# V of the first four tiles from x as loaded, and a new order of the V stage, in a fused attention and SwiGLU kernel

## The chip, the cores and the metric

The kernel runs on one core of one Trainium2 chip. Time is device time in microseconds of one execution; lower is better. A core has a matmul engine (PE, whose weight loads are shown as PEld), a vector engine (DVE), a scalar engine (ACT), GpSimd (POOL), and SyncE (SP), which here issues every DMA.

## What is computed

x has 2048 tokens of 640 elements, bf16. It is normalised once, and two branches are added to it: a linear attention with 32 heads of 20 elements and the feature map phi, and a SwiGLU with 1536 hidden columns.

```python
def _A_ref(x, wqkv, w_phi, wo):
    qkv = ...                      # x @ wqkv as q, k, v of (B, H, S, Dh)
    pq = jnp.einsum("bhsd,hdf->bhsf", q, w_phi)
    pk = jnp.einsum("bhsd,hdf->bhsf", k, w_phi)
    phi_q = jnp.concatenate([_softmax(pq), _softmax(-pq)], axis=-1)
    phi_k = jnp.concatenate([_softmax(pk), _softmax(-pk)], axis=-1)
    kv = jnp.einsum("bhsf,bhsd->bhfd", phi_k, v)
    z  = jnp.einsum("bhsf->bhf", phi_k)
    num = jnp.einsum("bhqf,bhfd->bhqd", phi_q, kv)
    den = jnp.einsum("bhqf,bhf->bhq", phi_q, z)[..., None] + 1e-6
    return ... (num / den) ... @ wo

def _B_ref(x, w1, w3, w2):
    return jnp.einsum("bsf,fd->bsd", _silu(x @ w1) * (x @ w3), w2)

xn = _layernorm(x)                 # (x - mean) / sqrt(var + 1e-5) over the 640
return x + _A_ref(xn, A_wqkv, A_w_phi, A_wo) + _B_ref(xn, B_w1, B_w3, B_w2)
```

## The kernel before

**Tiles and stages.** The tokens are 16 tiles of 128 rows. The order in which each engine meets its instructions is written out by hand: the engines run their own lists in order, and wait for one another by semaphores. Each operation below appends its instructions to the lists of the engines that it uses. The stages are named here after the first product that each makes.

- *V stage* (lines 642 to 734): x is loaded, normalised and transposed into `xnT` (640 elements as 5 chunks of 128 partitions, tokens along the row); V is computed tile by tile into `vaug`; six units of the SwiGLU are done between; and w_phi is folded into the K weights (`FB(d)`, five blocks, into `wkphi`).
- *K stage* (lines 737 to 749): 16 turns, one tile each. `phi_unit` makes ten matmuls `pk`, six exponentials on ACT, sums and reciprocals on DVE, and the division on POOL; `kv_unit` adds phi and V of the tile two turns back into `acc`; `fill` runs SwiGLU units. In turns 4 to 8 `fuse` folds w_phi into the Q weights.
- *Q stage* (lines 753 to 782): the same with `pq`; SwiGLU units in its first four turns, then the output of a tile per turn. SP transposes phi and o by DMA.

**Normalising a tile.** `ln_stats` (DVE, two bn_stats and one bn_aggr) gives mean and variance in `mv`. For tiles 0 to 3 `ln_root` takes a square root on ACT and `lx` begins with a reciprocal on DVE. For the others `ln_pow` and `ln_newton` make `rstd` on POOL, six small instructions for a pair of tiles. `ln_x` then writes (x - mean) * rstd in place, on DVE, or on ACT for tiles 12 and 13 (`BY_ACT`).

**Transposing a tile.** `T` is `x_transposed`. Tiles 0 to 3: five PE transposes into one PSUM bank and two copies by ACT into `xnT`. Tiles 4 to 15: one DMA transpose on SP. Each is behind its `ln_x`.

**V of a tile.** `V(t)` is ten matmuls at L304 (five chunks, each with 360 and 280 output columns in two banks), and three copies by ACT (L319) into `vaug`, which holds a column of ones ahead of each group of three heads.

**A SwiGLU unit** (sc, fi) is 512 tokens by 128 hidden columns: five matmuls into a bank `gp`, five into `up`, 512 columns each; a tanh on ACT; and two products on DVE (L436 reads `gp`, L439 reads `up`). `glu_half` makes half of the tokens. There are 48 units; the list `glu` gives their order, hidden columns 0 to 511 of all tokens first.

**PSUM.** Eight banks: one pair (`pair`, `two`), and six that are handed out as they come free (`bank`). An instruction that takes a bank waits for the last reader of its former content.

**SP** issues the loads in the order written, first x of tiles 0 and 1, then the V weights `wv` in three loads, then x of tiles 2 and 3. The first columns of w1 and w3 wait for a small POOL copy behind the root of tile 0 (L644), x of tiles 4 to 11 for one behind that of tile 1 (L649). The K weights come transposed by DMA in five pieces (`ldT(wkT, 1, d)`), one for each `FB(d)`. `wkT`, `wqT` and `wv` are the three parts of `reg_w`; `wo` is loaded over `wkT` when it is free.

Before tile 0 is there PE multiplies zeros (`warm(WARM)`, 44 matmuls of 128x128).

Of the kernel before, what the change touches and what calls it, by code (L numbers as in the profile page):

```python
# [8 lines left out]
P = 128  # L9
# [3 lines left out]
def kernel(  # L13
# [32 lines left out]
    BY_ACT = (12, 13)  # L46
    WARM = 44
# [52 lines left out]
    )  # L100
    vaug = reg_v[:, 0 : NST * NCH * VC].rearrange("p (t c e) -> p t c e", t=NST, e=VC)
# [11 lines left out]
    wide = one.tile([P, H * 21], f32, name="wide")  # L113

# [12 lines left out]
    with tc.manual_schedule():  # L127
# [20 lines left out]
        ld_wv(0, 1)  # L148
        ld_wv(1, 2)
        ld_wv(3, 2)  # L150
# [59 lines left out]
        def ln_stats(t, between=None):  # L210
            xt = xin[:, (t // 4) % 3, t % 4, :]
            st = work.tile([P, 2, 6], f32, name="st")
            for i in range(2):
                nc.vector.bn_stats(out=st[:, i, :], in_=xt[:, i * HD : (i + 1) * HD])  # L214
                if i == 0 and between:
                    between()
            nc.vector.bn_aggr(out=mv[:, t, :], in_=st[:])

        ry = one.tile([P, NST], f32, name="ry")
        shift = one.tile([P, NST], f32, name="shift")  # L220
# [16 lines left out]
        def ln_newton(t, n):  # L237

            r = slice(t, t + n)
            eng = nc.gpsimd  # L240
            if n == 1:
                eng.tensor_scalar(
                    out=rstd[:, r], in0=ry[:, r], scalar1=ve[:, r], scalar2=ry[:, r],
                    op0=ALU.mult, op1=ALU.mult,
                )
            else:
                eng.tensor_mul(out=rstd[:, r], in0=ry[:, r], in1=ry[:, r])
                eng.tensor_mul(out=rstd[:, r], in0=rstd[:, r], in1=ve[:, r])
            eng.tensor_scalar(
                out=rstd[:, r], in0=rstd[:, r], scalar1=-0.5, scalar2=1.5,  # L250
                op0=ALU.mult, op1=ALU.add,
            )
            eng.tensor_mul(out=rstd[:, r], in0=rstd[:, r], in1=ry[:, r])
            if t in BY_ACT:
                eng.tensor_scalar(
                    out=shift[:, r], in0=mv[:, r, 0], scalar1=rstd[:, r], scalar2=-1.0,
                    op0=ALU.mult, op1=ALU.mult,
                )

        def ln_x(t):  # L260
            xt = xin[:, (t // 4) % 3, t % 4, :]
            if t in BY_ACT:
                nc.scalar.activation(
                    out=xt, in_=xt, func=AF.Identity,
                    scale=rstd[:, t : t + 1], bias=shift[:, t : t + 1],
                )
                return
            nc.vector.tensor_scalar(
                out=xt, in0=xt, scalar1=mv[:, t, 0:1], scalar2=rstd[:, t : t + 1],
                op0=ALU.subtract, op1=ALU.mult,  # L270
            )

        def x_transposed(*ts, between=None):

            for t in ts:
                xn = xin[:, (t // 4) % 3, t % 4, :]
                if t >= BY_DMA:
                    nc.sync.dma_start_transpose(out=xnT[:, :, t * P : (t + 1) * P], in_=xn)
                    continue
                ps = bank("pst", bf)  # L280
                for c in range(KD):
                    nc.tensor.transpose(  # L282
                        ps[:, c * P : (c + 1) * P], xn[:, c * P : (c + 1) * P], ident[:]
                    )
                for c0, c1 in ((0, 2), (2, KD)):
                    nc.scalar.copy(  # L286
                        out=xnT[:, c0:c1, t * P : (t + 1) * P],
                        in_=ps[:, c0 * P : c1 * P].rearrange("p (c s) -> p c s", s=P),
                    )
                    if c0 == 0 and between:  # L290
                        between()
# [4 lines left out]
        def by_token(cols, w, name, cut, between=(KD, None)):  # L296

            ps = [bank(name), bank(name)]
            for c in range(KD):
                if c == between[0]:  # L300
                    between[1]()
                for i in range(2):
                    a, b = (0, cut) if i == 0 else (cut, D)
                    nc.tensor.matmul(  # L304
                        ps[i][:, 0 : b - a],
                        xnT[:, c, cols],
                        w[:, c, a:b],
                        start=(c == 0),
                        stop=(c == KD - 1),
                        skip_group_check=True,  # L310
                    )
            return ps

        def v_unit(dst, cols, between=(KD, None)):
            for piece in chunks(by_token(cols, wv, "pv", CH, between)):
# [102 lines left out]
        def glu_half(i, sc, fi, gp, up, between=None):  # L418

            for ps, w in ((gp, w1), (up, w3)):  # L420
                for c in range(KD):
                    nc.tensor.matmul(  # L422
                        ps[:, i * 256 : (i + 1) * 256],
                        w[:, c, fi * P : (fi + 1) * P],
                        xnT[:, c, sc * 512 + i * 256 : sc * 512 + (i + 1) * 256],
                        start=(c == 0),
                        stop=(c == KD - 1),
                        skip_group_check=True,
                    )
                if between:  # L430
                    between()
                between = None
# [175 lines left out]
        def stats(t0, n):  # L608
            for t in range(t0, t0 + n):
                ln_stats(t)  # L610
# [20 lines left out]
        def V(t, between=(KD, None)):  # L631
            v_unit(vaug[:, t], tile_of(t), between)
# [8 lines left out]

        ln_stats(0)
        ln_root(0)
        nc.gpsimd.tensor_copy(out=w1[0:1, 0, 0:1], in_=ry[0:1, 0:1])  # L644
        ld_glu(0, 256)
        ln_stats(1, between=lambda: lx(0, 1))
        T(0, between=lambda: ln_root(1))
        warm(4)
        nc.gpsimd.tensor_copy(out=xin[0:1, 1, 0, 0:1], in_=ry[0:1, 1:2])  # L649
        ld_tiles(4, 2)  # L650
        ld_tiles(6, 2)
        ld_tiles(8, 2)
        ld_tiles(10, 2)
        ld_glu(256, 512)
        ld(wps[:], A_w_phi.rearrange("h j f -> (h j) f").rearrange("(c p) f -> p c f", p=P))
        lx(1, 1)
        ln_stats(2)

        def second():
            T(1)  # L660
            ln_root(2)

        V(0, between=(4, second))
        ln_stats(3, between=lambda: lx(2, 1))
        pieces = list(chunks(by_token(tile_of(1), wv, "pv", CH)))
        v_copy(vaug[:, 1], *pieces[0])
        ln_root(3)


        first = (*glu.pop(0), *two("g0"))  # L670
        glu_half(0, *first, between=lambda: T(2))
        for piece in pieces[1:]:
            v_copy(vaug[:, 1], *piece)
        lx(3, 1)
        V(2, between=(3, lambda: T(3)))
        nc.scalar.activation(out=table[:], in_=nought[:, 0:1], func=AF.Tanh)
        ld_tiles(12, 4)
        ldT(wkT, 1, 0)
        pieces = list(chunks(by_token(tile_of(3), wv, "pv", CH)))
        stats(4, 2)  # L680
        stats(6, 2)
        glu_half(1, *first)
        g0 = glu_done(*first)
        for piece in pieces:
            v_copy(vaug[:, 3], *piece)
        lx(4, 2)
        T(4, 5)
        g1 = unit()
        g0()
        lx(6, 2)  # L690
        T(6, 7)
        ldT(wkT, 1, 1)
        stats(8, 1)
        stats(9, 1)
        g2 = unit()
        g1()
        lx(8, 1)
        T(8)
        g3 = unit(two("g3"))
        g2()  # L700
        lx(9, 1)
        T(9)
        ldT(wkT, 1, 2)
        V(4)
        V(5)
        stats(10, 2)
        g3()
        V(6)
        V(7)
        stats(12, 1)  # L710
        stats(13, 1)
        g4 = unit()
        lx(10, 2)
        T(10, 11)
        V(8)
        g4()
        stats(14, 2)
        lx(12, 1)
        T(12)
        V(9)  # L720
        g5 = unit()
        lx(13, 1)
        T(13)
        ldT(wkT, 1, 3)
        V(10)
        phi_blocks()
        g5()
        lx(14, 2)
        T(14, 15)
        ldT(wkT, 1, 4)  # L730
        V(11)
        ld_glu(512, F)
        nc.sync.dma_start_transpose(out=wqT, in_=A_wqkv[:, 0:D])
        V(12), FB(0), FB(1), V(13), FB(2), V(14), FB(3), V(15), FB(4)


        acc = pair("pkv")
        for t in range(NST):
            phi_unit(t, wkphi, "pk")
            if t > 1:  # L740
                kv_unit(t - 2, vaug[:, t - 2], acc, t == 2, False)
            if t:
                fill(1)
            if 4 <= t < 9:
                fuse(wqphi, wqT, t - 4, [bank("pf"), bank("pf")])
            fill(1)
            if t >= 12:
                norm_unit(wkphi, 0, t - 12)
# [4 lines left out]
        for t in range(NST + 4):  # L753
            if t < NST:
                phi_unit(t, wqphi, "pq")
            if t < 2:
                kv_unit(NST - 2 + t, vaug[:, NST - 2 + t], acc, False, t == 1)
# [3 lines left out]
            if t < 4:  # L761
                fill(3 if t else 2)
# [74 lines left out]
```

## Time and profile before

| | us |
|---|---|
| median of 3 runs | 270.27 (269.98 to 270.28) |
| span of the profiled execution | 268.56 |
| PE busy | 263.1 |
| DVE busy | 188.7 |
| ACT busy | 111.6 |
| POOL busy | 95.6 |
| first transpose of tile 0 on PE | 5.72 |
| first matmul of the K stage | 44.62 |
| first matmul of the Q stage | 139.67 |

The times of the table come from one profiled execution, but for the first row; its span ends with the last instruction, and the runs' median lies 1.71 us above it. The views used below list groups of instructions: the start in us from the span's start, the time from the start of the first to the end of the last of the group, the engine, the line of the kernel, the operation with what it writes and reads (out<-in), the count, and in brackets the idle time of the engine before it with what ended it. Matmuls overlap: the time of a group of them includes the tail of the last one.

### The profile page before, as it was taken

The page shows a single profiled execution, that of the slowest core. Times are in us where ns is not written, and L with a number is a line of the kernel's source. Part 1 is how long each engine was busy: PE and PEld are TensorE (multiplying, and loading weights), DVE is VectorE, ACT ScalarE, POOL GpSimd, SP SyncE. Part 2 cuts the span into 40 slices and gives each one's busy share as a digit, 9 for nine tenths or more (in the row PEclk, how much of TensorE's full clock was granted, in tenths as well). Part 3 has the DMA queues.
Part 4 walks back from the last instruction along what each step waited for, and adds up shares of the span by engine and source line. Part 5 has one row for each costly group of instructions (what it writes and reads, how often), then busy time and mean ns, then how long its engine had stood idle before and what let it go on. Part 6 is the DMA issues. An engine that isn't in the chain of part 4 may idle for free.

```text
span 268.6 us, 5257 instructions
## 1 busy us (share of the span) xinstructions
PE 263.1 (98%) x1979; PEld 167.9 (63%) x1996; DVE 188.7 (70%) x348; ACT 111.6 (42%) x342; POOL 95.6 (36%) x99
## 2 busy tenths in 40 slices
PE   8999999999999999999999999999999999999995
PEld 8656667555555555555555445677777777777773
DVE  4899950887776667777777788876766777776341
ACT  2673668544555554346656545422222222221000
POOL 5054740354433333334444321333344444433000
PEclk9999999999999999999999999999999999999999
DMA  6998347970000000000000874355556655556831
GB/s 213 324 219 147 84 100 208 278 200 2 0 0 2 0 4 0 0 4 0 0 2 0 240 164 99 75 136 128 130 133 125 151 128 128 129 144 136 155 98 55
DMA packets 62909, 27.81 MB, mean 104 GB/s; under 512 B 49952, under 2 KB 61600, under 8 KB 62880
## 3 DMA queue, kind: packets, MB, share of 16 engines
q1 hardware_dynamic: 62880, 27.43, 42.2%
q8 instruction: 17, 0.28, 0.4%
q14 instruction: 12, 0.10, 0.1%
HBM read 12.81 MB, written 2.62 MB: 57 GB/s over the span
## 4 chain that ended last, share of the span: by engine, by line
PE 97%; ACT 1%; issue 0%; DVE 0%
PE acc L547 28%; PE up L404 19%; PE gp L404 18%; PE pv L304 8%; PE pq L304 8%; PE pk L304 8%; PE pr L484 2%; PE pkv L449 2%; PE idle L193 2%; PE pf L388 1%; PE g L422 1%; PE g L404 1%; PE pst L282 1%; ACT reg_v L319 0%; ACT xnT L286 0%
## 5 line engine op out<-in xcount | busy, mean ns | idle before, releaser
L370 POOL TENSOR_TENSOR phi<-phi,rk 128x1320 bf16<-128x1320 bf16 x32 | 77.3, 2415 | 133.4 <-DVE rk L369 94.8
L367 DVE TENSOR_REDUCE sk<-phi 128x66 f32<-128x1320 bf16 x32 | 48.9, 1528 | 40.8 <-ACT phi L333 39.7
L404 PEld LDWEIGHTS <-w 128*128 128x128 bf16 x470 | 44.6, 98 | 49.4
L304 PEld LDWEIGHTS <-xnT 128*128 128x128 bf16 x480 | 45.3, 98 | 21.6 <-ACT xnT L286 1.6
L404 PE MATMUL up<-xnT,w 128*128 128x512 bf16 x227 | 57.0, 379 | 0.3
L404 PE MATMUL gp<-xnT,w 128*128 128x512 bf16 x216 | 55.9, 378 | 0.6
L547 PE MATMUL acc<-reg_v,reg_h 128*128 128x320 bf16 (+2 forms) x384 | 54.9, 299 | 0.0
L333 ACT ACTIVATE phi<-pq 128x360 bf16<-128x360 f32 (+2 forms) x96 | 24.8, 364 | 58.0 <-issue 44.1
L547 PEld LDWEIGHTS <-reg_h 128*128 128x128 bf16 x384 | 37.3, 98 | 14.4
L415 ACT ACTIVATE th<-gp 128x512 f32<-128x512 f32 x46 | 27.7, 603 | 30.2 <-PE gp L404 29.7
L439 DVE SCALAR_TENSOR_TENSOR reg_h<-gs,up 128x512 bf16<-128x512 bf16 x46 | 31.7, 688 | 5.1 <-PE pk L304 0.5
L333 ACT ACTIVATE phi<-pk 128x360 bf16<-128x360 f32 (+2 forms) x96 | 24.8, 364 | 24.1 <-PE pk L304 24.1
L436 DVE SCALAR_TENSOR_TENSOR gs<-th,gp 128x512 bf16<-128x512 f32 x46 | 30.2, 658 | 0.0
L556 DVE TENSOR_TENSOR res<-acc,xr 128x320 bf16<-128x320 f32 (+2 forms) x32 | 14.3, 487 | 20.3 <-PE acc L547 20.3
L304 PE MATMUL pk<-wkphi,xnT 128*128 128x360 bf16 (+1 forms) x160 | 24.5, 299 | 0.0
L547 PE MATMUL acc<-reg_w,reg_v 128*128 128x320 bf16 (+2 forms) x160 | 24.5, 299 | 0.0
L304 PE MATMUL pq<-wqphi,xnT 128*128 128x360 bf16 (+1 forms) x160 | 24.3, 299 | 0.0
L304 PE MATMUL pv<-reg_w,xnT 128*128 128x360 bf16 (+1 forms) x160 | 23.7, 300 | 0.4 <-ACT xnT L286 0.4
L369 DVE RECIPROCAL rk<-sk 128x66 f32<-128x66 f32 x32 | 18.1, 566 | 3.2
L547 PEld LDWEIGHTS <-reg_v 128*128 128x128 bf16 x160 | 15.7, 98 | 6.1
L319 ACT CAST reg_v<-pv 128x360 bf16<-128x360 f32 (+2 forms) x48 | 13.3, 354 | 6.5 <-PE pv L304 6.3
L214 DVE BATCH_NORM_STATS2 st<-reg_h 128x6 f32<-128x320 bf16 x32 | 13.9, 470 | 2.0 <-DMA reg_h<-in_A_x_dram 2.0
(72 smaller groups left out, 145.6 us busy)
## 6 DMA issues: line engine op xcount, KB each, us to landing
w<-in_B_w_dram SPq DMA_DIRECT2D x2, 1280.0 KB, 8.7
xr<-in_A_x_dram SPq DMA_DIRECT2D x16, 160.0 KB, 2.5
out_dram<-res SPq DMA_DIRECT2D x15, 160.0 KB, 1.8
reg_v<-in_B_w_dram SPq DMA_DIRECT2D x1, 1920.0 KB, 9.1
w<-in_B_w_dram SPq DMA_DIRECT2D x4, 320.0 KB, 5.6
reg_h<-in_A_x_dram SPq DMA_DIRECT2D x4, 320.0 KB, 4.7
reg_w<-in_A_wo_dram SPq DMA_DIRECT2D x1, 800.0 KB, 4.6
reg_h<-in_A_x_dram SPq DMA_DIRECT2D x4, 160.0 KB, 3.6
```

The source lines that it names most:

```text
L214: nc.vector.bn_stats(out=st[:, i, :], in_=xt[:, i * HD : (i + 1) * HD])
L304: nc.tensor.matmul(ps[i][:, 0 : b - a], xnT[:, c, cols], w[:, c, a:b], start=(c == 0), stop=(c == KD - 1), skip_group_check=True,)
L333: nc.scalar.activation(out=dst[:, c0 : c0 + n, g, 0:k], in_=p.rearrange("p (c f) -> p c f", c=n), func=AF.Exp, scale=1.0 - 2.0 * g,)
L367: nc.vector.reduce_sum(out=sk[:], in_=rows, axis=AX.X)
L369: nc.vector.reciprocal(out=rk[:], in_=sk[:])
L370: nc.gpsimd.tensor_mul(out=rows, in0=rows, in1=rk[:, :, :, None].to_broadcast([P, 2 * NCH, 3, Dh]))
L404: nc.tensor.matmul(ps, w[:, c, fi * P : (fi + 1) * P], xnT[:, c, sc * 512 : (sc + 1) * 512], start=(c == 0), stop=(c == KD - 1),)
L415: nc.scalar.activation(out=th[:], in_=gp, func=AF.Tanh, scale=0.5)
L436: nc.vector.scalar_tensor_tensor(out=gs[:], in0=th[:], scalar=1.0, in1=gp, op0=ALU.add, op1=ALU.mult)
L439: nc.vector.scalar_tensor_tensor(out=hT[:, 4 * sc : 4 * sc + 4, fi, :], in0=gs[:].rearrange("p (t s) -> p t s", t=4), scalar=0.5, in1=up.r ...
L547: nc.tensor.matmul(ps[:, 0 : b - a], rows[j][0], rows[j][1][:, a:b], start=(j == 0), stop=(j == len(rows) - 1),)
L556: nc.vector.tensor_tensor(out=res[:, a:b], in0=ps[:, 0 : b - a], in1=xr[:, a:b], op=ALU.add)
```

## The change

The V weights act on x as loaded for tiles 0 to 3: V = rstd * (x @ wv) - rstd * mean * (column sums of wv). So these tiles are transposed by PE without being normalised (`by_pe(xrT, t)`, into the part of `reg_w` that later holds `wqT`), multiplied (`raw_part`), and scaled by rstd into `v_raw`, on DVE for tile 0 and on ACT for tiles 1 to 3. The second term is added in the K stage: wv is loaded a second time, transposed, over `wkT`; in turns 4 to 8 ACT sums its rows with a minus sign (`column_sum`); SP writes the 640 sums to DRAM and reads them back to all partitions (`less_sum`); in turns 10 to 13 DVE adds them, times `drift` = mean * rstd, to `v_raw` into `vaug` (`raw_centred`). The K stage therefore takes tiles 4 to 15 first and 0 to 3 last.

For the SwiGLU and for K and Q the tiles 0 to 3 are still normalised and transposed: 0, 1 and 3 by PE a second time, tile 2 by DMA. 19 matmuls of zeros are left of 44 ahead of the first transpose. The V stage has eight SwiGLU units in place of six, the first two by halves side by side, and turns 2 and 3 of the Q stage one unit less each. Tiles 12 and 13 are normalised on DVE like the others. `ln_stats` of two tiles makes its four bn_stats before its two bn_aggr. The V weights come in five loads; the loads of w1, w3, x, w_phi and the transposed K weights have a new order, and so have the units, tiles and blocks of the V stage. V of every second tile takes the pair of banks.

```diff
-    BY_ACT = (12, 13)
-    WARM = 44
+    WARM = 19
+    RAW = 4
...
+    xrT = reg_w[:, KD * D : KD * D + KD * RAW * P].rearrange("p (c s) -> p c s", c=KD)
+    v_raw = one.tile([P, RAW, D], f32, name="v_raw")
+    less_sum = wide[:, 0:D]
...
-        ld_wv(0, 1)
-        ld_wv(1, 2)
-        ld_wv(3, 2)
+        for c in range(KD):
+            ld_wv(c, 1)
...
+        def by_pe(dst, t):
+            xt = xin[:, (t // 4) % 3, t % 4, :]
+            ps = bank("pst", bf)
+            for c in range(KD):
+                nc.tensor.transpose(
+                    ps[:, c * P : (c + 1) * P], xt[:, c * P : (c + 1) * P], ident[:]
+                )
+            for c0, c1 in ((0, 2), (2, KD)):
+                nc.scalar.copy(
+                    out=dst[:, c0:c1, t * P : (t + 1) * P],
+                    in_=ps[:, c0 * P : c1 * P].rearrange("p (c s) -> p c s", s=P),
+                )
+
+        def raw_part(t, c, ps):
+            for i, (a, b) in enumerate(((0, CH), (CH, D))):
+                nc.tensor.matmul(
+                    ps[i][:, 0 : b - a],
+                    xrT[:, c, t * P : (t + 1) * P],
+                    wv[:, c, a:b],
+                    start=(c == 0),
+                    stop=(c == KD - 1),
+                    skip_group_check=True,
+                )
+
+        def raw_scaled(t, ps):
+            for i, (a, b) in enumerate(((0, CH), (CH, D))):
+                nc.scalar.activation(
+                    out=v_raw[:, t, a:b], in_=ps[i][:, 0 : b - a],
+                    func=AF.Identity, scale=rstd[:, t : t + 1],
+                )
+
+        def raw_scaled_dve(t, ps, i):
+            a, b = ((0, CH), (CH, D))[i]
+            nc.vector.tensor_scalar(
+                out=v_raw[:, t, a:b], in0=ps[i][:, 0 : b - a],
+                scalar1=rstd[:, t : t + 1], scalar2=None, op0=ALU.mult,
+            )
+
+        def column_sum(c):
+            junk = work.tile([P, D], bf, name="junk")
+            nc.scalar.activation(
+                out=junk[:], in_=wkT[:, c], func=AF.Identity, scale=-1.0,
+                accum_out=sums[:, c : c + 1],
+            )
+
+        def raw_centred(t):
+            for c0, n, k in ((0, 10, 60), (10, 1, 40)):
+                cols = slice(60 * c0, 60 * c0 + k * n)
+                nc.vector.scalar_tensor_tensor(
+                    out=vaug[:, t, c0 : c0 + n, 1 : 1 + k],
+                    in0=less_sum[:, cols].rearrange("p (c e) -> p c e", c=n),
+                    scalar=drift[:, t : t + 1],
+                    in1=v_raw[:, t, cols].rearrange("p (c e) -> p c e", c=n),
+                    op0=ALU.mult, op1=ALU.add,
+                )
...
+        by_pe(xrT, 0)
+        warm(4)
         ln_stats(0)
         ln_root(0)
...
+        by_pe(xrT, 1)
+        ln_stats(1)
+        ln_root(1)
+        vps = [two("v0"), [bank("pv"), bank("pv")]]
+        lx(0, 1)
+        for c in range(2):
+            raw_part(0, c, vps[0])
+            raw_part(1, c, vps[1])
+        T(0)
+        raw_part(0, 2, vps[0])
+        raw_part(1, 2, vps[1])
+        lx(1, 1)
+        T(1)
+        raw_part(0, 3, vps[0])
+        raw_part(1, 3, vps[1])
+        raw_part(0, 4, vps[0])
+        by_pe(xrT, 2)
+        raw_part(1, 4, vps[1])
+        ld_glu1(w1, B_w1, 0, 256)
         nc.gpsimd.tensor_copy(out=xin[0:1, 1, 0, 0:1], in_=ry[0:1, 1:2])
         ld_tiles(4, 2)
+        ld_glu1(w3, B_w3, 0, 256)
         ld_tiles(6, 2)
+        ln_stats(2)
+        ln_root(2)
+        by_pe(xrT, 3)
+        ln_stats(3)
+        ln_root(3)
+        lx(2, 1)
+        by_dma(2)
+        ld_glu(256, 512)
         ld_tiles(8, 2)
         ld_tiles(10, 2)
...
+        raw_scaled(1, vps[1])
         lx(3, 1)
+        raw_scaled_dve(0, vps[0], 0)
+        raw_scaled_dve(0, vps[0], 1)
...
+        T(3)
+        (sc, fa), (_, fb) = glu.pop(0), glu.pop(0)
...
         stats(4, 2)
         stats(6, 2)
...
         lx(4, 2)
+        by_dma(4)
+        by_dma(5)
+        ld_tiles(12, 2)
         g0()
+        g2 = unit()
         lx(6, 2)
+        by_dma(6)
+        by_dma(7)
+        ld_tiles(14, 2)
+        ld(wps[:], A_w_phi.rearrange("h j f -> (h j) f").rearrange("(c p) f -> p c f", p=P))
+        g1()
+        stats(8, 2)
+        g3 = unit()
+        g2()
+        V(4)
+        g3()
+        lx(8, 2)
+        by_dma(8)
+        by_dma(9)
+        V(5, two("pv"))
+        stats(10, 2)
+        V(6)
+        stats(12, 2)
+        V(7, two("pv"))
+        ldT(wkT, 1, 0)
+        lx(10, 2)
+        by_dma(10)
+        by_dma(11)
+        g4 = unit()
+        g4()
+        g5 = unit()
+        g5()
         ldT(wkT, 1, 1)
+        lx(12, 2)
+        by_dma(12)
+        by_dma(13)
+        V(8)
+        stats(14, 2)
+        V(9, two("pv"))
+        phi_blocks()
+        V(10)
+        V(11, two("pv"))
         ldT(wkT, 1, 2)
+        lx(14, 2)
+        by_dma(14)
+        by_dma(15)
         ldT(wkT, 1, 3)
         ldT(wkT, 1, 4)
+        g6 = unit()
+        FB(0)
+        g6()
+        V(12)
+        FB(1)
         ld_glu(512, F)
         nc.sync.dma_start_transpose(out=wqT, in_=A_wqkv[:, 0:D])
+        V(13)
+        g7 = unit()
+        g7()
+        FB(2)
+        V(14)
+        FB(3)
+        FB(4)
+        V(15)
+
+        turns = [*range(RAW, NST), *range(RAW)]
         acc = pair("pkv")
-        for t in range(NST):
+        for i, t in enumerate(turns):
             phi_unit(t, wkphi, "pk")
...
+            if i == 0:
+                nc.sync.dma_start_transpose(out=wkT, in_=A_wqkv[:, 2 * D : 3 * D])
+            if 4 <= i < 9:
+                column_sum(i - 4)
+            if i == 9:
+                ld(row[:].rearrange("c p -> p c"), sums[:])
+                ld(less_sum, row[:].rearrange("c p -> (c p)").partition_broadcast(P))
+            if 10 <= i < 10 + RAW:
+                raw_centred(i - 10)
...
-                fill(3 if t else 2)
+                fill(3 if t == 1 else 2)
```

## The prediction

> **What bounds the kernel now.** I read the busy shares, then the chain that ended last, then the order of time on PE at the start, then on DVE and POOL through the V stage. First the page (span, busy shares, chain by engine):
>
> ```profile
> span 268.6 us, 5257 instructions
> PE 263.1 (98%) x1979; PEld 167.9 (63%) x1996; DVE 188.7 (70%) x348; ACT 111.6 (42%) x342; POOL 95.6 (36%) x99
> ...
> PE 97%; ACT 1%; issue 0%; DVE 0%
> ```
>
> PE sets the end. A change can only take away PE work, or time in which PE does nothing useful; such time lies at the start (PE in order of time: start, length, what, count):
>
> ```profile
> 1.05 4.87 PE L193 MATMUL idle<-nought 128*128 128x128 bf16 x44 [1.05 <-DVE nought L189]
> 5.72 0.73 PE L282 MATMUL pst<-ident,reg_h 128*128 128x128 bf16 x5
> 6.91 1.28 PE L304 MATMUL pv<-reg_w,xnT 128*128 128x360 bf16 x8 [0.24 <-ACT xnT L286]
> ...
> 8.03 0.44 PE L282 MATMUL pst<-ident,reg_h 128*128 128x128 bf16 x5
> ...
> 16.17 1.03 PE L404 MATMUL gp<-xnT,w 128*128 128x512 bf16 x4
> ...
> 44.62 1.72 PE L304 MATMUL pk<-wkphi,xnT 128*128 128x360 bf16 x10
> ```
>
> PE multiplies zeros until 5.72, because tile 0 must be normalised before it is transposed. The same five transposes take 0.73 at 5.72 and 0.44 at 8.03: 0.107 us each, then 0.056; the rate doubles near 6.3 in the starts of single matmuls, though the clock row prints full speed throughout. From 16 on PE has no gap. The L404 group at 16.17 shows 4 of 5 matmuls, so it began one matmul (0.216) earlier, at 15.95. The ten pk matmuls at 44.62 take 1.72 instead of the 1.52 of their group elsewhere: 0.20 of waiting.
>
> The V stage on DVE, and on POOL, which makes rstd:
>
> ```profile
> 3.00 0.89 DVE L214 BATCH_NORM_STATS2 st<-reg_h 128x6 f32<-128x320 bf16 x2 [2.01 <-DMA reg_h<-in_A_x_dram]
> 4.13 0.49 DVE L214 BATCH_NORM_STATS2 st<-reg_h 128x6 f32<-128x320 bf16 x1
> 13.91 0.25 POOL L225 TENSOR_SCALAR ve<-mv 128x2 f32<-128x2 f32 x1 [6.62 <-DVE mv L217]
> 15.88 0.20 POOL L253 TENSOR_TENSOR rstd<-rstd,ry 128x2 f32<-128x2 f32 x1
> 16.16 0.22 POOL L225 TENSOR_SCALAR ve<-mv 128x2 f32<-128x2 f32 x1
> 26.72 0.63 DVE L436 SCALAR_TENSOR_TENSOR gs<-th,g 128x512 bf16<-128x512 f32 x1
> 27.39 0.69 DVE L439 SCALAR_TENSOR_TENSOR reg_h<-gs,g 128x512 bf16<-128x512 bf16 x1
> 34.11 0.94 DVE L379 TENSOR_TENSOR wphi<-wps,mask 128x800 bf16<-128x800 bf16 x1
> 34.28 0.86 POOL L225 TENSOR_SCALAR ve<-mv 128x2 f32<-128x2 f32 x1 [0.20 <-DVE mv L217]
> 37.08 0.80 DVE L268 TENSOR_SCALAR reg_h<-reg_h,mv,rstd 128x640 bf16<-128x640 bf16 x2 [0.64 <-POOL rstd L253]
> ```
>
> x of tiles 0 and 1 is there at 3.0 and 4.1. A pair's rstd takes POOL 2.17 (13.91 to 16.08) after the sums, but 2.8 where its first step falls beside phi_blocks (34.28 to 37.05).
>
> **The change, step by step.** Times are on the span's clock; each wait named is one in the built program of the changed kernel.
>
> *Start.* 19 idle matmuls end at 3.05, when x of tile 0 is there. Raw transposes of tile 0 to 3.58, 4 idle to 4.01, tile 1 at 4.14 (x) to 4.67. A raw part (360 and 280 columns) costs 0.27 at the full rate (1.36 for the five of a tile) and 0.53 before. Three, with 0.12 of waiting for ACT's copy of tile 1, end at 6.36. The other seven for tiles 0 and 1 (1.90) and four rounds of transposes (4 x 0.28) end at 9.38; tiles 2 and 3 (2.72, 0.07 of waiting for ACT) at 12.17, T(3) at 12.45, four half products (5 x 0.109 each) at 14.63. That is the V work of four tiles and one unit's halves, which took until 15.95: **1.32 ahead**, with 15 more transposes inside. wv in five loads puts two more issues (0.5 each) on SP ahead of tiles 2 and 3, but the bytes ahead of them are the same: they landed at 7.5 and 8.0 and are wanted at 8.5 and 9.1. Tiles 4 and 5 wait for POOL's copy behind the root of tile 1 (5.9), w1's first columns for nothing; the loads are backed up past 8 either way. Without waits the K stage would start at 44.62 + 4.32 (two units moved here, 10 x 0.216 each) - 1.32 = 47.62, and the 0.20 of waiting at 44.62 goes: at best 1.5 gained.
>
> *What DVE can follow.* ACT now carries twelve copies (128x256 and 128x384, 0.27 and 0.36 apart) ahead of the root of tile 3, which comes at 10.8, so lx(3) starts at 11.04 (0.36). The two scalings of tile 0 on DVE aren't in the trace; a PSUM read of 128x360 is 0.39 apart in kv_done, so 0.78 (0.7 to 0.9): 12.2. ACT's scalings, bounded by the 128x360 copy (0.35) and the 128x512 tanh (0.60), free tile 1's banks by 11.6, wanted at 12.17. stats(4) ends 2.1 later (11.71 to 13.82), POOL's chain at 16.56, that of tiles 6 and 7 at 18.77. From lx(6) at 18.80: lx of a pair 0.72, a product 1.35 (26.72 to 28.00 is 1.28, elsewhere up to 1.39), stats of a pair 2.02, some 0.05 less grouped. lx(6), g1, stats(8), g2, g3, lx(8), stats(10) make 9.43: 28.23; rstd 30.62, behind which stats(12) hides; lx(10), g4, g5, lx(12), stats(14) make 6.11: 36.76. phi_blocks again stands right behind stats(14): rstd at 39.77, lx(14) to 40.49, g6's first product to 41.24, its second to 41.93.
>
> V(13) takes the two banks of g6. PE would be there at 40.43 (47.62 less V(13), g7, FB(2), V(14), FB(3), FB(4), V(15): 4.07 + 2.16 + 0.95); its second matmul must wait until 41.97 instead of 40.58: **1.39 lost**. K starts at 49.01.
>
> *SP.* A transpose occupies SP 1.25 and lands after 2.5, those of the weights after 2.9 to 3.6. by_dma(2) lands near 13.1, before 14.63. by_dma(10) and (11) land at 33.6 and 34.85, V(10) and V(11) start at 33.6 and 34.96: nothing to spare. ldT 3 and 4, moved behind by_dma(15), are issued from 42.9 and land at 45.9 and 47.2; FB(4) starts at 47.35. wqT, and the added load of wv's transpose behind it (10.85 of SP each), end near 69; the first column_sum comes near 76. wo, moved behind the column sums, is wanted after 160.
>
> *K stage.* Per turn DVE idles 1.08 and ACT 1.78 before the next exponentials (rows at 112.72 and 111.14). raw_centred (640 elements; 0.69 for 512, 0.94 for 800): 0.76 to 1.0, I take 0.9, in four turns; column_sum: 0.86 + 0.19 as the square of 128x800, in five. Both fit. If they didn't, products end 1.1 before their bank is used again. The store and the load of the sums (2.5 each, as xr, to 6.5, as wps, which queued behind others) have two turns, over 12 us, with DMA idle. In the Q stage two turns lose a unit each; w2 lands 18 us after that stage begins and is wanted 9 us later: nothing. Moved products cost DVE the same there and here.
>
> **Sum**: 48.94 + 0.20 - 49.01 = 0.13 less. The profiled 268.56 becomes 268.43; the median of the runs stands 1.71 above it, so **270.1**. 0.2% of 270.27 (0.54) is about what a measurement of this kernel can tell from none, so this is no change: the early start is real and DVE's queue gives it back.
>
> The row at 34.28 has POOL's step held by a DVE product with two inputs in SBUF. The Trainium skill (SBUF — State Buffer, Who interferes with whom) says the two share a port pair, held for a whole instruction, also by fast two-port forms such as lx. By that rule POOL's second chain would be held by lx(4) and all behind be 0.6 later: 270.7. The row at 16.16, 0.22 beside an lx, disagrees; I keep the sum.
>
> **Rivals.**
> 1. *DVE keeps up.* Each 0.1 off its chain is 0.1 off the end, until V(13) no longer waits: 268.8 at best. For: six products at 1.28 give 0.4, phi_blocks missing POOL's step another 0.6; together 269.1. Against: the same order had it caught before. 0.30, near 269.3.
> 2. *The rate of the matmuls doubles at another time.* Real work now lies before 6.3. With the switch at 7.8 the next parts at 0.53 put tile 3's transposes and the chain some 0.6 later: 270.7; at 4.6 the loads limit PE and the gain is 0.6: 269.5. One switch is seen, so nothing says it is fixed. 0.10, of it 0.06 early. The Trainium skill (TensorE: Matmul & The Clock Gate, Part 1) has the half rate end after a busy window of 3.4 us whose phase is free; by that rule both cases occur, and this trace's one switch neither agrees nor contradicts.
> 3. *Slower: DVE's chain is longer.* Place: DVE from lx(6) to g6, where it never idles but for rstd. Products with 0.79 between their halves (22.77 to 23.56) give 6 x 0.13 = 0.8, four stats at 2.02 another 0.2: 271.1. It decides from 0.67 more than my chain; past that each delay reaches FB(4) as well through ldT 4. 0.16.
> 4. *The additions of the K stage don't fit* (a write of 640 four-byte pieces later than two turns, or raw_centred over 1.1 + 1.08): a wait of 0.5 to 1 for DVE's banks, 271.0. 0.06.
> 5. The sum as it stands, 269.7 to 270.7: 0.38.
>
> **Numbers.** Faster 0.30 + 0.06 = 0.36; within 0.54 0.38 + 0.04 = 0.42; slower 0.22. The likeliest's own range is 269.7 to 270.7; 269.0 to 271.2 leaves out the far ends of 1, 3 and 4, about 0.2.
>
> **What would show it.** Right: raw transposes at 3.05, the first full unit at 16.8, V(13) waiting over 1 us for DVE's product, pk first at 49.0, no gap in PE behind. Wrong in the start: T of tile 3 raw later than 9.5. Wrong in the chain: lx(14) far from 39.8, or the wait at V(10) or FB(4) instead. Wrong altogether: gaps of PE in the K stage.

## The result, and the profile after

The changed kernel takes 270.63 us (270.06 to 271.18, 13 runs) against 270.09 (269.57 to 270.39, 13 runs) for the kernel before beside it: a ratio of 1.0021, with a 95% interval of 1.0013 to 1.0029. Run once more among the experiments it took 271.23 against 270.11: 1.0039 (1.0026 to 1.0052). So it is slower, by 0.54 and 1.12 us, where 0.13 less was forecast.

The page of the changed kernel (span; busy time; the queue of instruction loads with packets, MB and share; the chain that ended last, by engine):

```profile
span 269.1 us, 5283 instructions
PE 262.1 (97%) x1977; PEld 167.2 (62%) x1996; DVE 192.6 (72%) x360; ACT 115.2 (43%) x350; POOL 91.9 (34%) x89
...
q14 instruction: 11, 0.09, 0.2%
...
PE 83%; DVE 9%; POOL 3%; DMA 2%; issue 2%; SPq 1%; DVEq 0%
```

The chain that was 97% PE now runs through DVE, POOL and DMA for a seventh of the span: that is the V stage. PE at its start, in order of time:

```profile
3.05 0.74 PE L283 MATMUL pst<-ident,reg_h 128*128 128x128 bf16 x5
...
7.68 0.43 PE L294 MATMUL v<-reg_w 128*128 128x360 bf16 x2 [0.42 <-DMA reg_w<-in_A_wqkv_dram]
...
9.14 0.44 PE L283 MATMUL pst<-ident,reg_h 128*128 128x128 bf16 x5
...
12.85 0.71 PE L461 MATMUL g<-xnT,w 128*128 128x256 bf16 x5 [0.19 <-DVE v_raw L312]
...
17.32 1.04 PE L444 MATMUL gp<-xnT,w 128*128 128x512 bf16 x3
```

The raw transposes begin at 3.05, tile 3's end at 9.42 (forecast 9.38), and the first full unit begins at 17.32 at the latest (forecast 16.8; the first ones of its group are missing from the trace in part). PE waits for a chunk of wv and for a bank that DVE empties. Then V(13), DVE and PE together, in the changed kernel:

```profile
40.03 0.80 DVE L265 TENSOR_SCALAR reg_h<-reg_h,mv,rstd 128x640 bf16<-128x640 bf16 x2 [2.01 <-POOL rstd L261]
40.74 0.68 DVE L472 SCALAR_TENSOR_TENSOR gs<-th,gp 128x512 bf16<-128x512 f32 x1
41.48 0.31 PE L344 MATMUL pv<-reg_w,xnT 128*128 128x360 bf16 x1 [0.33 <-DVE gs L472]
41.53 0.69 DVE L475 SCALAR_TENSOR_TENSOR reg_h<-gs,up 128x512 bf16<-128x512 bf16 x1
42.27 1.37 PE L344 MATMUL pv<-reg_w,xnT 128*128 128x280 bf16 x9 [0.48 <-DVE reg_h L475]
...
49.35 1.52 PE L344 MATMUL pk<-wkphi,xnT 128*128 128x360 bf16 x10
```

lx(14) and lx(15) wait 2.01 for rstd; the two products of g6 stand behind them, and V(13) takes g6's banks: two waits on PE. By the starts of the matmuls, less what one takes in a row of its like, they cost 0.49 + 0.64 = 1.13. K starts at 49.35. From there to the last matmul's start PE takes 216.09. Before the change it took as much: 265.24 - 49.14 = 216.10, where 49.14 is the first pk matmul of the kernel before, 44.62, with the 4.32 of the two moved units and the 0.20 of waiting that is in its first group. From the last matmul's start to the end of the span the changed kernel takes 3.69, against 3.32.

### The profile page after: what moved, and what is told of

Same layout as the page of the kernel before. It is cut to its first block, busy times and chain, and to the rows that moved or that the text cites. A ratio compares the mean times of both kernels' runs of the same rounds, so it can differ in the third digit from the quotient of the medians.

```text
span 269.1 us, 5283 instructions
## 1 busy us (share of the span) xinstructions
PE 262.1 (97%) x1977; PEld 167.2 (62%) x1996; DVE 192.6 (72%) x360; ACT 115.2 (43%) x350; POOL 91.9 (34%) x89
## 4 chain that ended last, share of the span: by engine, by line
PE 83%; DVE 9%; POOL 3%; DMA 2%; issue 2%; SPq 1%; DVEq 0%
PE acc L583 27%; PE up L444 16%; PE gp L444 16%; PE pq L344 8%; PE pk L344 8%; DVE st L223 3%; PE pr L520 2%; PE pkv L485 2%; DMA reg_h<-in_A_x_dram 2%; DVE reg_h L265 2%; DVE reg_h L475 2%; PE pv L344 2%; DVE gs L472 1%; SPq L125 1%; POOL ry L236 1%
## 5 line engine op out<-in xcount | busy, mean ns | idle before, releaser
L444 PEld LDWEIGHTS <-w 128*128 128x128 bf16 x460 | 43.5, 98 | 48.3 <-DMA w<-in_B_w_dram 0.5
L344 PEld LDWEIGHTS <-xnT 128*128 128x128 bf16 x440 | 41.8, 98 | 19.9 <-issue 1.1
L455 ACT ACTIVATE th<-gp 128x512 f32<-128x512 f32 x47 | 28.3, 602 | 30.0 <-PE gp L444 29.5
L475 DVE SCALAR_TENSOR_TENSOR reg_h<-gs,up 128x512 bf16<-128x512 bf16 x47 | 32.3, 688 | 5.2 <-DVE gs L472 0.5
L472 DVE SCALAR_TENSOR_TENSOR gs<-th,gp 128x512 bf16<-128x512 f32 x47 | 30.9, 658 | 3.2 <-ACT th L455 3.2
L344 PE MATMUL pv<-reg_w,xnT 128*128 128x360 bf16 x120 | 17.4, 299 | 0.8 <-DVE reg_h L475 0.5
L541 DVE TENSOR_TENSOR o__77<-pr,den 128x360 bf16<-128x360 f32 (+1 forms) x32 | 14.2, 486 | 0.6
```

The lines of the kernel that those rows point to most:

```text
L344: nc.tensor.matmul(ps[i][:, 0 : b - a], xnT[:, c, cols], w[:, c, a:b], start=(c == 0), stop=(c == KD - 1), skip_group_check=True,)
L444: nc.tensor.matmul(ps, w[:, c, fi * P : (fi + 1) * P], xnT[:, c, sc * 512 : (sc + 1) * 512], start=(c == 0), stop=(c == KD - 1),)
L455: nc.scalar.activation(out=th[:], in_=gp, func=AF.Tanh, scale=0.5)
L472: nc.vector.scalar_tensor_tensor(out=gs[:], in0=th[:], scalar=1.0, in1=gp, op0=ALU.add, op1=ALU.mult)
L475: nc.vector.scalar_tensor_tensor(out=hT[:, 4 * sc : 4 * sc + 4, fi, :], in0=gs[:].rearrange("p (t s) -> p t s", t=4), scalar=0.5, in1=up.r ...
```

## The experiments

Each was timed beside the kernel before. All medians are in us; "chain of the sums" is the time from the issue of their store to the landing of `less_sum`; "K to Q end" is from the first pk matmul to the last matmul of the kernel, "closing" from there to the end of the span, all in the profiled execution.

| run | median | ratio to before (95%) | lost at V(13), at FB(4) | pk first | chain of the sums | K to Q end | closing |
|---|---|---|---|---|---|---|---|
| changed | 270.63 | 1.0021 (1.0013 to 1.0029) | 1.13, 0 | 49.35 | 15.31 | 216.09 | 3.69 |
| g6_first | 270.23 | 1.0014 (1.0003 to 1.0025) | 0, 0.92 | 49.28 | 13.90 | 216.10 | 3.68 |
| ldT_first | 270.19 | 1.0012 (1.0003 to 1.0020) | 0.87, 0 | 48.59 | 13.84 | 216.10 | 3.68 |
| both_moved | 269.52 | 0.9987 (0.9977 to 0.9997) | 0, 0 | 47.82 | 14.75 | 216.09 | 3.68 |
| no_sums | 270.25 | 1.0010 (1.0001 to 1.0019) | 1.46, 0 | 48.65 | none | 216.09 | 3.43 |
| pool_plus_one | 270.65 | 1.0017 (1.0007 to 1.0028) | 1.19, 0 | 48.98 | 16.11 | 216.70 | 3.33 |
| three_wv | 271.28 | 1.0042 (1.0027 to 1.0057) | 0.78, 0 | 49.16 | 15.99 | 216.58 | 3.73 |
| warm_44 | 273.08 | 1.0108 (1.0094 to 1.0123) | 1.24, 0.86 | 51.62 | 16.35 | 216.94 | 3.68 |
| x23_by_act | 271.45 | 1.0073 (1.0044 to 1.0102) | 1.06, 0 | 48.97 | 15.87 | 216.46 | 3.68 |
| changed_again | 271.23 | 1.0039 (1.0026 to 1.0052) | 1.16, 0 | 49.00 | 15.84 | 216.43 | 3.68 |
| centred_later | 270.52 | 1.0016 (1.0007 to 1.0025) | 1.05, 0.18 | 49.44 | 16.36 | 216.09 | 3.68 |
| three_mended | 268.99 | 0.9966 (0.9953 to 0.9979) | 0, 0 | 47.41 | 16.15 | 216.09 | 3.33 |
| pool_plus_four | 270.9, one run | none | 1.01, 0 | 49.13 | 16.05 | 216.64 | 3.32 |

### The place around V(13): g6_first, ldT_first, both_moved

g6_first puts all five lines from lx(14) to ldT 4 behind g6's products; ldT_first only puts the two ldT ahead of lx(14). both_moved does both:

```diff
-        lx(14, 2)
-        by_dma(14)
-        by_dma(15)
         ldT(wkT, 1, 3)
         ldT(wkT, 1, 4)
         g6 = unit()
         FB(0)
         g6()
+        lx(14, 2)
+        by_dma(14)
+        by_dma(15)
```

g6_first:

> In the changed kernel g6's two products stand on DVE behind lx(14) and lx(15), which wait 2.01 us for POOL's rstd, and V(13) loses 1.13 us on PE to them (gaps of 0.49 and 0.64). Here lx(14), lx(15), their two transposes and the weight transposes ldT 3 and 4 stand behind g6's products. Theory A (two queues meet here: DVE's at V(13), and right behind it SP's at FB(4)): g6's second product ends near 40.15 instead of 42.22 and V(13) no longer waits, but ldT 4, still issued near 44.4 and landing near 47.7, now holds FB(4) for about 1.1 us; pk first at 49.3 to 49.5, time 270.5 to 270.8, as the changed kernel's 270.63. Rival B (DVE's queue alone sets this place): pk first at 48.2, 269.5. Rival C (the loss has nothing to do with these waits and lies in the closing): neither the V stage nor the time moves.

ldT_first:

> The changed kernel with ldT 3 and 4 ahead of lx(14) and of the transposes of tiles 14 and 15 on SP; DVE's order as it was. Theory A: V(13) goes on waiting 1.1 us for g6's product, FB(4) no longer comes close to a wait (ldT 4 lands near 44.8 instead of 47.62); pk first near 49.3, 270.4 to 270.7. Rival B' (SP's queue alone sets this place): pk first near 48.2, 269.5. A transpose of tile 14 that comes too late for V(14) would show as a gap at V(14), up to 0.5.

both_moved:

> Both moves in the changed kernel: ldT 3 and 4 first on SP, then g6 with its products, then lx(14), lx(15) and their transposes. Theory A: no gap at V(13) and none at FB(4); transposes of tiles 14 and 15 land near 44.3 and 45.6, wanted at 44.8 and 46.8; pk first at 48.2 instead of 49.35, time 270.63 - 1.13 = 269.5, under the kernel before (270.09). Rival C (the loss is not in this place, or a fourth wait takes over at V(14) or V(15)): pk first at 48.8 or later, 270.1 or more.

With g6's products first, V(13) waits no more, but FB(4) loses 0.92 by the starts of the matmuls: K starts at 49.28, no earlier. FB(4) in g6_first:

```profile
47.59 0.49 PE L428 MATMUL pf<-wphi,reg_w 128*128 128x140 bf16 x6 [0.76 <-ACT wkphi L437]
```

The view names ACT's copies of the block before, but in the changed kernel FB(4) follows FB(3) without a break, ahead of these copies; ldT 4, which FB(4) reads, lands at 47.55. With the weight transposes first V(13) still loses 0.87; K starts at 48.59, but this profile had a start 0.7 quicker (lx(6) at 18.43 for 19.09), which DVE's chain kept. The times of the two, 270.23 and 270.19, lie under what Theory A gave (270.5 to 270.8 and 270.4 to 270.7), and their intervals overlap that of the changed kernel: here the profiles decide, not the times. With both, DVE and PE in both_moved:

```profile
38.41 0.69 DVE L472 SCALAR_TENSOR_TENSOR gs<-th,gp 128x512 bf16<-128x512 f32 x1 [1.03 <-ACT th L455]
39.20 0.69 DVE L475 SCALAR_TENSOR_TENSOR reg_h<-gs,up 128x512 bf16<-128x512 bf16 x1
39.80 0.80 DVE L265 TENSOR_SCALAR reg_h<-reg_h,mv,rstd 128x640 bf16<-128x640 bf16 x2
40.65 1.52 PE L344 MATMUL pv<-reg_w,xnT 128*128 128x360 bf16 x10
...
45.84 0.79 PE L428 MATMUL pf<-wphi,reg_w 128*128 128x140 bf16 x12
```

The products fill the time in which DVE waited for rstd, lx(14) starts at 39.80 all the same, V(13) runs its ten matmuls without a break, and so do FB(3) and FB(4). K starts at 47.82, and the time is 269.52. That start is 1.53 earlier than in the changed kernel: 1.13 are the waits, and the other 0.40 goes with a quicker start (lx(6) at 18.49), which is luck of the execution. Theory A holds: two waits stood one behind the other, and mending either alone gives nothing in the V stage.

### The sums: no_sums

```diff
-            if i == 0:
-                nc.sync.dma_start_transpose(out=wkT, in_=A_wqkv[:, 2 * D : 3 * D])
-            if 4 <= i < 9:
-                column_sum(i - 4)
-            if i == 9:
-                ld(row[:].rearrange("c p -> p c"), sums[:])
-                ld(less_sum, ...)
+        nc.gpsimd.memset(less_sum, 0.0)      # once, ahead of the turns
```

> The changed kernel without wv's transposed load, the five column sums on ACT and the store and load of the sums; the row that is subtracted is zeros, so V of tiles 0 to 3 is left without its mean (raw_centred still runs). Theory A: the additions of the K stage are hidden, since PE shows no gap there: 270.5 to 270.8, as the changed kernel. Rival D (they cost, by ACT's time or by the 8 us store of 640 pieces, something that the records of PE don't show, or hold the closing): 270.1 or less.

270.25 lies between the two. PE's 216.09 in the K and Q stages is that of the changed kernel, but the closing is shorter, 3.43 for 3.68, and this kernel has one more instruction on GpSimd. So it does not separate the sums from the closing: that made two questions of one.

### The closing: pool_plus_one, pool_plus_four

```diff
         acc = pair("pkv")
+        spare = one.tile([P, 1], f32, name="spare")
+        nc.gpsimd.memset(spare[:], 0.0)      # four of these in pool_plus_four
```

pool_plus_one:

> The changed kernel with one more instruction on GpSimd, a memset of 128x1 just ahead of the K stage, of no use. From the last matmul's start to the end of the span the kernel before took 3.32 us, the changed one 3.69 and its three variants with the sums 3.68 each; 0.31 of it lies between two steps of GpSimd's closing (267.845 to 267.930 before, 268.053 to 268.452 after). The kernel without the sums took 3.43, but had one more instruction on GpSimd too (the memset of the zeros). Theory F (where GpSimd's closing steps lie in its stream of instructions decides): the step takes 0.09 again, last matmul to end 3.3 to 3.45, time 270.2 to 270.4. Theory G (the sums, their store or their DMA's closing hold it): 0.40 stays, 3.68, 270.5 to 270.8.

pool_plus_four:

> The changed kernel with four more instructions on GpSimd ahead of the K stage, to see how the step in its closing depends on the position: 0.40 with none added, 0.09 with one. If the position counts in groups of four, 0.40 again, and 3.68 from the last matmul to the end; if it is a rarer place in the stream, 0.09 and 3.33. It says nothing of the other two losses.

The page of pool_plus_one, and its last instruction on DVE; then the last of the changed kernel:

```profile
span 269.0 us, 5303 instructions
...
q14 instruction: 12, 0.10, 0.2%
...
266.00 0.42 DVE L592 TENSOR_TENSOR res<-acc,xr 128x256 bf16<-128x256 f32 x1 [1.30 <-PE acc L583]
```

```profile
265.75 0.42 DVE L592 TENSOR_TENSOR res<-acc,xr 128x256 bf16<-128x256 f32 x1 [1.30 <-PE acc L583]
```

pool_plus_one's last result comes 0.25 later, and its span ends 0.1 earlier. The step of GpSimd's closing takes 0.09 in it and in pool_plus_four, and 0.39 to 0.40 in all nine profiles with the changed kernel's GpSimd list. Theory F holds for this step, but not in groups of four. The row of the instruction loads goes with it: 11 packets in all nine, 12 or 13 in the five others, the kernel before among them. These five load a block of instructions between 247 and 255 us, after GpSimd's last branch, that the nine do not. The Trainium skill (Runtime: NRT & Kernel Launch, Instruction fetch mechanics) says that a taken branch whose target is not in the loaded blocks stalls until it is fetched. No row here shows that GpSimd waits for that block, or for which engine it is loaded: that the number of GpSimd's instructions sets the step is shown, by what way is open.

pool_plus_one's time did not fall, though: 270.65, where 270.2 to 270.4 was expected. Its K and Q stages took 0.61 more; the next section has the reason.

### The row of sums: changed_again, centred_later

```diff
-            if 10 <= i < 10 + RAW:
-                raw_centred(i - 10)
+            if 11 <= i < 11 + RAW:               # centred_later
+                raw_centred(i - 11)
```

changed_again:

> The changed kernel once more, as the measure for the runs beside it and for how much its own profile varies. In the last four profiles the chain of the sums (issue of their store to landing of the row) took 15.9 to 16.4 us, against 13.9 to 15.3 in the first ones, and PE lost 0.37 to 0.85 near 122 us, which it did not in the first ones. Theory K (the sums' way through DRAM is at its limit: raw_centred of tile 0 waits for it on DVE, the products behind it are late, and PE waits for their bank as soon as that chain takes more than about 15.5): time 270.5 to 270.8, the loss near 122 is there if the chain takes over 15.5, not there if it takes less. Rival (that loss belongs to the four kernels run together, not to the changed kernel): none here, whatever the chain takes.

centred_later:

> The changed kernel with raw_centred one turn of the K stage later (turns 11 to 14 instead of 10 to 13); nothing else moves. Theory K: the row of sums has 5.8 us more, DVE does not wait for it, PE has no gap near 122, pk's first matmul to the last matmul is 216.1 in every profile; the time is under that of the changed kernel beside it by what that loses near 122, 0.2 to 0.6 in the median: 270.1 to 270.4. Rival (DVE's own time for raw_centred, 1.0 a turn, is the trouble, wherever it stands): a gap of as much one turn later, near 128, or in turn 14, where a sum of norms stands too; 270.5 to 270.8.

The chain of waits of changed_again in this stretch (start, length, what):

```profile
102.69 8.79 issue
111.48 6.62 DMA wide<-row
...
118.12 1.02 DVE reg_v L327 x2
119.14 1.45 DVE sk L407
...
120.68 0.57 DVE rk L409
121.25 0.56 DVE gs L472
...
121.84 1.24 PE gp L444 x5
```

The store of the sums, issued at 102.26, lets the load go at 111.48 (the 8.79 for which the chain has no name), and the row lands at 118.10. In order of time:

```profile
118.12 1.02 DVE L327 SCALAR_TENSOR_TENSOR reg_v<-wide,drift,v_raw 128x600 bf16<-128x600 f32 x2 [2.31 <-DMA wide<-row]
119.06 1.52 DVE L407 TENSOR_REDUCE sk<-phi 128x66 f32<-128x1320 bf16 x1
...
121.84 1.24 PE L444 MATMUL gp<-xnT,w 128*128 128x512 bf16 x5 [0.18 <-DVE gs L472]
```

raw_centred of tile 0 waits 2.31 at the head of DVE's list; the sums of phi, the reciprocal and a SwiGLU product behind it are late, and PE waits for the bank that this product reads. The starts of the matmuls give a loss of 0.33. In the changed kernel's first profile the same instruction waited less, and PE not at all:

```profile
117.95 1.02 DVE L327 SCALAR_TENSOR_TENSOR reg_v<-wide,drift,v_raw 128x600 bf16<-128x600 f32 x2 [1.78 <-DMA wide<-row]
```

Over the runs with raw_centred in turn 10, the excess of "K to Q end" over 216.09 is the chain of the sums less 15.5, to 0.01: 15.84 gives 0.33, 15.87 0.37, 15.99 0.49, 16.05 0.54, 16.11 0.61, 16.35 0.85, and under 15.5 nothing. A turn later, in centred_later, raw_centred starts without a wait:

```profile
122.18 1.01 DVE L327 SCALAR_TENSOR_TENSOR reg_v<-wide,drift,v_raw 128x600 bf16<-128x600 f32 x2
```

There a chain of 16.36 costs nothing (216.09), and the time is 270.52 beside 271.23. Theory K holds for the loss on PE. Both times lie above what it gave (270.5 to 270.8 and 270.1 to 270.4), and they differ by 0.71, more than the 0.33 that the profile of changed_again lost; the other executions have no profile.

### The start: three_wv, warm_44, x23_by_act

```diff
-        for c in range(KD):
-            ld_wv(c, 1)
+        ld_wv(0, 1); ld_wv(1, 2); ld_wv(3, 2)          # three_wv
...
-    WARM = 19
+    WARM = 44                                          # warm_44
...
+        for t in (2, 3):                               # x23_by_act: not by SP
+            nc.scalar.dma_start(out=xin[:, 0, t], in_=x2[t * P : (t + 1) * P, :])
```

three_wv:

> The changed kernel with wv in three loads (1, 2 and 2 chunks) as before the change, instead of five; two issues fewer ahead of x of tiles 2 and 3. Theory E (the two added issues put x of tiles 2 and 3 off, and DVE's chain with them): x of tile 3 lands near 8.0, as before the change, instead of 8.5 to 9.1; lx(3) near 10.2 instead of 10.6 to 11.4, pk 0.4 to 0.5 earlier at 48.2 to 48.9, time 270.1 to 270.3. Rival (the bytes set the landings, and their spread between executions is larger than what two issues are worth): x of tile 3 lands at 8.4 or later, time 270.5 to 270.8.

warm_44:

> The changed kernel with 44 idle matmuls instead of 19, so that the first transposes of x come at 5.7 as before the change and not at 3.05. Theory A (the early start is real and works through the roots of tiles 2 and 3 on DVE's chain to V(13)): T of tile 3 raw about 0.8 later, lx(3) and all behind it too, V(13) still waits, time 271.2 to 271.5. Rival H (the loads set the start anyway: the parts wait for wv's chunk 3 at 6.1 to 7.6 and T(2) for x at 7.7 to 8.5): 270.6 to 270.9.

x23_by_act:

> The changed kernel with x of tiles 2 and 3 issued on ACT's queue at the start, beside SP's, so that they stand behind no issue of wv. Theory I (SP's issues, one in 0.47 us, set the landings): all nine loads are there by 8.0, lx(3) near 10.2 or earlier, time 270.1 to 270.3. Theory J (the bytes set them): x of tiles 2 and 3 land before 6, wv's chunks 3 and 4 near 8.5 to 9 as the last, parts on PE wait for them, lx(3) as now at 10.6 or later, time 270.5 to 270.9.

three_wv puts the landings of x of tiles 2 and 3 back to 7.49 and 7.96, and yet lx(3) comes at 11.31: its chunks 1 and 2 of wv land together at 6.25, PE waits 0.57 for them, and what is behind is as late as before. So in this profile the five loads give to PE what they take from x. x23_by_act has all nine loads there by 7.51, and lx(3) at 11.17; x of tile 0 lands 0.66 later (3.67), with the load of tile 2 now beside it. Neither theory's account of lx(3) held: what stands ahead of it is PE's work on tiles 0 to 2, ACT's copies and its roots, and moving one or two loads did not bring it forward; which of these sets it is not shown. Both times, 271.28 and 271.45, lie above what either theory gave; their profiles lose 0.49 and 0.37 near 122, as in the section before. The six runs of x23_by_act reach from 270.92 to 273.40, and why is open.

warm_44 is 1.8 us worse than changed_again, far over what was expected; its profile is of its slowest run. V of tiles 2 and 3 starts at 11.23 instead of 9.0 to 9.7, so DVE's whole chain is 1.7 later than in changed_again, and ldT 4, behind lx(14), now lands at 49.88 and costs FB(4) 0.86 besides: K starts at 51.62. The early start is worth more than the 0.8 that I gave it.

### The three losses together: three_mended

both_moved, pool_plus_one and centred_later in one kernel:

> The three in one: g6's products and the weight transposes first (as in both_moved), one more instruction on GpSimd ahead of the K stage, and raw_centred a turn later. If the three losses (1.1 to 1.2 at V(13) and FB(4), 0.36 in the closing, 0 to 0.6 near 122) stand one behind the other on PE's way to the end, they add up: pk near 47.8 to 48.0, pk to last matmul 216.1, last matmul to end 3.33, time 269.0 to 269.2, faster than the kernel before by 0.8 to 1.1. Rival (they overlap, or one of them comes back elsewhere): 269.4 or more, as both_moved alone.

```profile
span 266.8 us, 5303 instructions
PE 262.7 (98%) x1996; PEld 167.6 (63%) x1996; DVE 193.1 (72%) x360; ACT 115.2 (43%) x350; POOL 91.8 (34%) x90
...
q14 instruction: 12, 0.10, 0.2%
...
PE 98%; DVE 0%; issue 0%
...
120.15 1.01 DVE L327 SCALAR_TENSOR_TENSOR reg_v<-wide,drift,v_raw 128x600 bf16<-128x600 f32 x2
```

268.99: faster than the kernel before by 0.34% (0.21 to 0.47) and than changed_again by 2.24. The profiles account for it: against changed_again K starts 1.59 earlier, the K and Q stages take 0.33 less and the closing 0.35. Of the 1.59, 1.16 is the wait at V(13); the rest goes with a quicker start (lx(3) at 10.65 for 11.18), so the three changes themselves are worth some 1.8. The chain is PE alone again, and raw_centred starts without a wait.

## Why the prediction was wrong, point by point

- *What bounds it.* Right: PE, with the V stage tied to DVE's queue.
- *Start.* The times of PE held (9.42 for 9.38). Wrong in a detail: x of tiles 2 and 3 did not keep 7.5 and 8.0 ("the bytes ahead of them are the same"), but landed at 7.5 to 8.5 and 8.1 to 9.3 over the profiles with five loads. three_wv shows that this was not what made the kernel slower.
- *What DVE can follow.* Right. lx(3), lx(6) and lx(14) were put at 11.04, 18.80 and 39.77; six profiles that leave the start and the order up to V(13) alone have 10.58 to 11.44, 18.22 to 19.09 and 39.13 to 40.03. The two scalings took 0.92 for 0.78, just above their bound of 0.9. POOL's first step beside an lx takes 0.22 again (at 16.93 and 31.09) and 0.84 beside the product of phi_blocks (at 37.25), so keeping the sum there was right. V(13) loses 1.0 to 1.5 where 1.39 was said. K starts at 48.65 to 49.44, mean 49.09, where 49.01 was said and 49.14 is as before: on average the V stage is no change, as the sum had it. One profile differs from the next by up to 0.8 here, so that the mean comes within 0.1 of the forecast is partly luck.
- *SP.* ldT 4 was put at 47.2 for a use at 47.35; it landed at 47.62. It was no cause, but it is why mending DVE's queue alone gains nothing.
- *K stage.* **The first step that failed**: "Both fit", and the store and load of the sums "have two turns, over 12 us, with DMA idle". DVE's own time was nearly right (1.02 for 0.76 to 1.0). The store took 8.6 to 9.6 from its issue until the load could go, where 2.5 to 6.5 was allowed, and the load 5.3 to 7.0. The load was not on idle engines, since wo stands next on SP and moves its 800 KB beside it; no run shows what it takes without wo. Together 13.8 to 16.4, at a limit of 15.5: a cost of 0 to 0.85, by the execution. In the first profile of the changed kernel (15.31) it was 0.
- *Closing.* **The second step that failed**: the sum carried all that lies behind the last matmul over from the kernel before and so put the change there at nothing, without a reason. It took 0.36 more (0.41 in three_wv) in all nine profiles with the changed GpSimd list, which is ten instructions shorter, and with one or four instructions added to that list nothing more.
- *The sum.* The changed kernel's first profile: +0.21 at pk (49.35 for 49.14), 0 in the K and Q stages, +0.37 in the closing make 0.57, the difference of the spans (269.13 and 268.56). changed_again: -0.14, +0.33 and +0.36 make 0.55 (269.11). As medians stand, 0.67 lies between 0.13 less and 0.54 more. The closing gives 0.36 of it. Another 0.18 lies in the kernel before: the profiled execution that the sum starts from, 270.27, is one of its slower ones, for a median of 270.09 over 13 runs. The 0.13 left is within the spread of the V and K stages. Why the medians beside changed_again differ by 1.12 is not shown, as its slower executions have no profile.
- *Rivals.* 4 came in part, at a chance of 0.06: the write that it named is late, and costs 0.33 to 0.85 (its price was 0.5 to 1) in six of the ten profiles with raw_centred in turn 10, and nothing in the other four, the changed kernel's first among them. The closing no rival had. 1 fell: DVE did not keep up; with the order mended (both_moved) the time is 269.52, where it said 269.3. 3 fell: DVE's chain was as long as said (lx(14) at 39.74 in the mean of the six). 2: the granted clock goes full between 4.0 and 6.8 us in thirteen profiles, so the switch does move, as the Trainium skill (TensorE: Matmul & The Clock Gate, Part 1) has it, though by more than the 0.5 us to either side that it gives. But K starts at 49.44 with the earliest switch and at 49.00 with one at 6.0, so it did not decide when K starts.

## What to carry to other kernels

A value that goes through DRAM to be spread must be wanted with room to spare: the wait of its first reader stands at the head of an in-order queue, and everything behind it pays. Where a step is freed from one queue, look at once for the next queue that meets the same place; two waits of equal length behind one another hide each other, and only both moves show a gain. A difference of some 0.3 us may lie behind the last matmul, in the closing, and go with nothing but the number of instructions on an engine that PE does not wait for, as the 0.36 here.

## What was unexpected of the hardware

The store of 640 four-byte pieces keeps the DMA engines busy for a moment only. The busy share of the 16 engines in changed_again from 102 to 118 us, in 40 slices of 0.4 us:

```profile
DMA  0007000000000000000050000000000685898889
```

The pieces pass from 103.2 to 103.6; then nothing moves but one block of instructions, from 110.2, until the load's first packets at 114.7. The load was issued at 111.48, so the 8 us behind the pieces is neither traffic nor queueing on these engines as far as they are recorded. That block of instructions took 3.2 to 4.2 us in all twelve profiles with the store, 0.44 in no_sums, and other blocks 0.3 to 1.0. What the store waits for, and why its chain took 13.8 to 15.3 in the first four profiles and 15.8 to 16.4 in the later ones, stays open. The chip may be the reason: g6_first, ldT_first and both_moved, where the store took 8.6, ran on one chip, and the eight later profiles, with 9.2 to 9.6, on two others. Which chip the changed kernel's first profile (9.3) ran on is not known, so no run separates the chip from the kernel.
